# The weight products of a two-branch transformer kernel: the rows of the last chunk computed for two heads at a time, the flips of that chunk merged, and the first loads cut into halves

## The chip, the cores and the metric

The kernel runs on one core of a Trainium2 chip. The core has five engines: TensorE (matrix products; the profile shows its products as PE and its weight loads as PEld), VectorE (DVE), ScalarE (ACT), GpSimd (POOL) and SyncE (SP, which here only issues transfers). Sixteen DMA engines move data between device memory and the on-chip memory. Products are accumulated in eight banks of PSUM, and DVE or ACT copy them out. The metric is the device time of one launch in microseconds. The kernel before takes 1566.67 us, the median of three runs from 1566.27 to 1566.87.

## The reference

The input x has 2048 tokens of width 448 in bfloat16. Two kinds of layers alternate, twice each, every one of them on a layer norm of x and added to x.

```python
x = x + A(layernorm(x));  x = x + B(layernorm(x))
x = x + A(layernorm(x));  x = x + B(layernorm(x))

def A(x):                          # 64 segments of 32 tokens, one after the other
    mem = mem0                     # 8 rows
    for s in range(64):
        h = concat([mem, x[segment s]])               # 40 rows
        q, k, v = h @ Wq, h @ Wk, h @ Wv              # 16 heads of 256
        p = softmax(mask(q @ k.T * 256 ** -0.5))      # memory rows see all, others are causal
        o = (p @ v) @ Wo                              # back to 448
        mem, out[s] = o[:8], o[8:]

def B(x):                          # 448 -> 1792 -> 448
    return (relu(x @ W_gate) * (x @ W_up)) @ W_down
```

Both A layers have the same weights, and so have both B layers. Layer A is a chain: each segment needs the memory rows of the one before.

## The kernel before, in words

**Preparation.** The weights of A are multiplied with each other first. For each head, A_h = Wq_h Wk_h^T is a matrix of 448 x 448, and B_h = Wv_h Wo_h is another. The scores are then (h A_h) h^T and the output is p (h B_h). `A_sb` and `B_sb` hold these products for all 16 heads. A width of 448 is three chunks of 128 (`kd` = 0, 1, 2) and one of 64 (`kd` = 3). The heads are worked through in eight pairs: a *position* `p` is two heads, `eo` = 0 and 1, of two 128-column pieces each; `hf, p4 = divmod(p, 4)`.

In the first loop over positions (lines 378 to 413) Wq and Wk of a position lie in memory as 448 rows by 512 columns. `load_nat` (306) asks for them on SP's queue: rows 0 to 383 as one transfer, rows 384 to 447 as a second one, and again 64 rows to the other half of the partitions (those of Wq once more, or of Wv beside Wk). TensorE flips them with transposes, 128 x 128 each, into a bank `tpw` (`flips`, 327; its `half` is one unit with eight transposes), and a copy takes them to `qT` or `kT`. The part of Wv that came with Wk is copied to `v3`. The units of position p+1 are kept in `todo` and are done between the products of position p. For each `kd` and `eo` two products of 384 columns go to a bank `aps` and two of 64 columns to `mxw` (388 to 393). At `kd` = 3 these products hold the same 64 rows of A in both halves of the partitions, and the copies take 64 rows to the lower or the upper half, as the main loop wants them (`upper`, 51). All four units of position 0 stand ahead of the first product.

In the second loop (415 to 441) B_sb is made: twelve transposes of Wv a position, twelve products of 448 columns into `bps`, and one group of four products with 64 output rows each, two and two side by side in the left and right columns of the array (431 to 435). Wo comes on POOL's queue (`load_wo`, 369), with a wait that spreads it over TensorE's work (`spread`, 88).

**Who copies.** `share` (320) keeps a clock of expected ends for DVE and ACT and gives each copy to the one that would be done first. `bank` (121) takes the bank that is expected to be free longest. TensorE's instructions are tied to the order in which they are written (`in_order`, 80). DVE's and ACT's are tied to it only from the main loop on (`dve.on = act.on = True`, 1047). Before that the scheduler of the framework may order them otherwise, and it did: the statistics of the first rows of x, written behind position 1, run at 2.80 us.

**Warm-up.** `keep_warm` (173) issues products on zeros while TensorE waits for the first load: eight at the start and four between the flips of Wq and of Wk of position 0.

**Main loop.** 68 steps, two chains (the first A layer, and the second four segments behind) in one step. A step projects h with all tiles of A (`project`, 639): 28 tiles for each of the halves `hf` = 0, 1, in banks of six, six, four, six and six tiles, each bank copied out to `TQ` (tiles 0 to 23) or `TZ` (24 to 27). `EARLY` (43) says which banks take their last chunk from the lower or the upper half of the partitions, two products side by side. `scores` (759) multiplies chunks of `TQ` and `TZ` with h; the order of chunks is `KD` (46), 0, 1, 3, 2, and for both chains the first three chunks of the memory's and of the own scores stand ahead of the last (788 to 792). Then come softmax, a flip of the weights p to `PT`, the products with h (`weigh_m`, `weigh_x`) into `Y`, and those with B_sb (`project_out`). Every other step also runs a block of layer B in between.

Of the kernel before, what the change touches and what calls it, by code (L numbers as in the profile page):

```python
# [15 lines left out]
DM = 448  # L16
# [26 lines left out]
EARLY = (((0, 6), (12, 18)), ((0, 6), (12, 18)))  # L43


KD = (0, 1, 3, 2)
# [4 lines left out]
def upper(hf, t):  # L51

    return any(b <= t < b + 6 for _, b in EARLY[hf])


def tidx(kd, eo, p4):

    return kd * 8 + eo * 4 + p4 if kd < 3 else 24 + p4


def build_kernel(ctx, tc, A_x, A_mem0, A_Wq, A_Wk, A_Wv, A_Wo, B_W_gate, B_W_up, B_W_down, out,
# [31 lines left out]
    class InOrder:  # L93

        def __init__(self, eng):
            self.eng, self.last, self.on = eng, None, False

        def __getattr__(self, name):
            f = getattr(self.eng, name)

            def call(*a, **k):
                r = f(*a, **k)  # L102
                if self.on:
                    if self.last is not None:
                        tc.add_manual_dep(r.ins, self.last,
                                          mybir.DependencyInfo(mybir.DependencyClass.NoSync,
                                                               mybir.DependencyReason.DATA),
                                          reason="order of issue")
                    self.last = r.ins.name
                return r  # L110

            return call
# [55 lines left out]
    nc.sync.dma_start(xp[1][:], x_dram[0:128])  # L168
# [124 lines left out]
    with tc.tile_pool(name="pre", bufs=6) as pre:  # L293
# [3 lines left out]
        nats = []  # L297
        for i in range(6):
            t = pre.tile([P, 4, 512], BF, name=f"nat{i}", bufs=1)
            nats.append(t)  # L300
        nc.gpsimd.memset(A_sb[64:128, 3, :, 24:NT, :], 0.0)
        for t in TQ + TZ + PX + PM + YB:
            nc.gpsimd.memset(t[:], 0.0)
        nn = [0]

        def load_nat(src, p, eng):
            t = nats[nn[0] % 6]
            nn[0] += 1
            cols = slice(512 * p, 512 * (p + 1))
            eng.dma_start(t[:, 0:3, :], src[0:384, cols].rearrange("(k p) n -> p k n", p=P))  # L310
            if src is Wv:
                return t
            eng.dma_start(t[0:64, 3, :], src[384:448, cols])
            eng.dma_start(t[64:128, 3, :], (Wq if src is Wq else Wv)[384:448, cols])
            return t

# [3 lines left out]
        def share(dst, src, n, per):  # L320
# [4 lines left out]
            evac(eng, dst, src)  # L325

        def flips(src, p, name):
            nat = load_nat(src, p, nc.sync)
            o = pre.tile([P, 4, 512], BF, tag="tT", name=name, bufs=4)

            def half(e2):
                tp = bank([P, 2, 512], BF, "tpw")
                n = 3 if src is Wv else 4
                for kd in range(n):
                    for e in range(2):
                        tr(tp[:, e, kd * 128:(kd + 1) * 128],
                           nat[:, kd, (2 * e2 + e) * 128:(2 * e2 + e + 1) * 128], ident[:])
                n = DM if src is Wk else 128 * n
                share(o[:, 2 * e2:2 * e2 + 2, 0:n], tp[:, :, 0:n], 2 * n, (0.6, 0.82))
                if src is Wk:  # L340
                    share(v3[:, p, 2 * e2:2 * e2 + 2, :], tp[:, :, DM:512], 128, (0.6, 0.82))

            return o, [lambda: half(0), lambda: half(1)]

        def queue(p):
            if p < NP:
                qT, a = flips(Wq, p, "qT")
                kT, b = flips(Wk, p, "kT")
                return (qT, kT), a + b
            if p == NP:  # L350
                return flips(Wv, 0, "vT")
            return None, []
# [13 lines left out]
        keep_warm(8)  # L366
# [5 lines left out]

        ready, todo = queue(0)
        for k, u in enumerate(todo):
            if k == 2:
                keep_warm(4)
            u()
        for p in range(NP):
            hf, p4 = divmod(p, 4)
            qT, kT = ready  # L380
            ready, todo = queue(p + 1)
            mx_ps = bank([P, 4, 128], F32, "mxw")
            for kd in range(4):
                for eo in range(2):
                    aps = bank([P, 3, 128], F32, "aps")
                    for t in range(2):
                        e = 2 * eo + t
                        mm(aps[:, :, :], qT[:, e, kd * 128:(kd + 1) * 128],
                           kT[:, e, 0:384], start=(t == 0), stop=(t == 1))
                    for t in range(2):  # L390
                        e = 2 * eo + t
                        mm(mx_ps[:, kd, eo * 64:eo * 64 + 64], qT[:, e, kd * 128:(kd + 1) * 128],
                           kT[:, e, 384:448], start=(t == 0), stop=(t == 1))
                    t0 = eo * 4 + p4
                    if kd < 3:
                        share(A_sb[:, kd, hf, t0:t0 + 17:8, :], aps[:], 384, (1.28, 0.85))
                    else:
                        up = [t for t in range(3) if upper(hf, t0 + 8 * t)]
                        for rows, ts in ((slice(64, 128), up), (slice(0, 64), [t for t in range(3) if t not in up])):
                            if ts:  # L400
                                d = ts[1] - ts[0] if len(ts) > 1 else 1
                                share(A_sb[rows, 3, hf, t0 + 8 * ts[0]:t0 + 8 * ts[-1] + 1:8 * d, :],
                                      aps[rows, ts[0]:ts[-1] + 1:d, :], 128 * len(ts), (1.28, 0.85))
                    if todo and 2 * kd + eo in (0, 2, 4, 5):
                        todo.pop(0)()
            share(A_sb[:, 0:3, hf, 24 + p4, :], mx_ps[:, 0:3, :], 384, (1.28, 0.85))
            share(A_sb[0:64, 3, hf, 24 + p4, :], mx_ps[0:64, 3, :], 128, (1.28, 0.85))
# [4 lines left out]
            if p == 2:  # L412
                first_rows(xn0)

        for p in range(NP):
            hf, p4 = divmod(p, 4)
            vT = ready
            ready, todo = flips(Wv, p + 1, "vT") if p + 1 < NP else (None, [])
            wo = wos.pop(0)
            for eo in range(2):  # L420
                for kd in range(3):
# [6 lines left out]
                    if kd == 1 and todo:  # L428
                        todo.pop(0)()
            bps = bank([P, 512], F32, "bps")  # L430
            for t in range(2):
                for eo in range(2):
                    e = 2 * eo + t
                    mm(bps[64 * eo:64 * eo + 64, 0:DM], v3[:, p, e, :], wo[:, e, :],
                       start=(t == 0), stop=(t == 1), tile_position=(0, 64 * eo))
            share(B_sb[:, hf, 24 + p4, 0:DM], bps[:, 0:DM], DM, (1.28, 0.85))
# [180 lines left out]
    def tile_of(ps, hf, t, i, chains, hb, j, kds, first, last):  # L617

        n = L * len(chains)
        for kd in kds:  # L620
            mm(ps[:, i * n:(i + 1) * n], A_sb[:, kd, hf, t, :], moving(hb, j, kd, chains),
# [522 lines left out]
```

## Time and profile before

| | |
|---|---|
| median of three runs | 1566.67 us |
| the profiled execution | 1565.94 us |
| its span on the core | 1564.1 us |
| TensorE busy | 1552.9 us (99%) |
| DVE, ACT, POOL busy | 1113.5, 759.1, 77.2 us |
| first product of the first loop, `aps` | at 9.26 us |
| first product of the second loop, `bps` | at 47.64 us |
| first product of the main loop, `prj` | at 75.23 us |

How to read the lines: an engine's group of instructions has its line in the kernel, the operation, what it writes and reads by the names of the kernel (`A_sb<-aps`), the shape and the count; then busy time and the mean duration of one in ns; then idle time of the engine before them and what ended it. In the timeline the first two numbers are start and length in us. Times count from the start of the span. Helpers hide the callers: nearly all products have line 144 and nearly all copies line 102, so the names of tiles tell them apart. The shown end of a product is some 0.16 us after the next one can start, because products are pipelined; the spacing of starts is the cost. In the chain of work, each piece is a start, a length and what it was.

### The profile page before, as it was taken

How to read it: one execution, taken by the hardware profiler on the slowest of the kernel's cores; microseconds unless marked ns; L12 is line 12 of the kernel's file. 1: busy time of each engine (PE TensorE's matmuls, PEld its weight loads, DVE VectorE, ACT ScalarE, POOL GpSimd, SP SyncE). 2: the span in 40 equal slices, each digit the busy share in tenths (PEclk: the TensorE clock that was granted, in tenths of full speed). 3: DMA queues.
4: the chain of work that ended last, by engine and by line, in shares of the span. 5: the costliest groups of instructions: out<-in, count | busy, mean ns of one | idle time of the engine just before them, and what ended most of it. 6: DMA issues, size and time to landing. Idle time of an engine off the chain costs nothing.

```text
span 1564.1 us, 89359 instructions
## 1 busy us (share of the span) xinstructions
PE 1552.9 (99%) x40988; PEld 1441.7 (92%) x40988; DVE 1113.5 (71%) x3656; ACT 759.1 (49%) x2126; POOL 77.2 (5%) x172
## 2 busy tenths in 40 slices
PE   9999999999999999999999999999999999999998
PEld 6689999999999999999999999999999999999997
DVE  8756777777767777777777777677777777777765
ACT  5744454454444445544444455444544554445444
POOL 3200000000000000000000000000000000000000
PEclk9999999999999999999999999999999999999999
DMA  7620000000000000000000000000000000000000
GB/s 247 199 85 9 8 10 9 7 7 10 9 9 9 10 10 4 9 9 10 9 10 9 10 3 10 9 10 9 9 9 10 4 9 9 10 8 6 7 7 9
DMA packets 28233, 33.21 MB, mean 21 GB/s; under 512 B 4168, under 2 KB 26960, under 8 KB 27856
## 3 DMA queue, kind: packets, MB, share of 16 engines
q1 hardware_dynamic: 26608, 23.76, 5.3%
q8 instruction: 320, 5.24, 1.4%
q0 software_dynamic: 1088, 3.68, 0.7%
q14 instruction: 57, 0.47, 0.1%
q10 hardware_dynamic: 160, 0.06, 0.0%
HBM read 23.70 MB, written 1.84 MB: 16 GB/s over the span
## 4 chain that ended last, share of the span: by engine, by line
PE 98%; DVE 1%; issue 0%; DMA 0%; SPq 0%; ACT 0%; POOL 0%; DVEq 0%; ACTq 0%
PE prj L144 32%; PE ox L144 25%; PE gps L144 6%; PE ups L144 6%; PE dps L144 6%; PE o L144 5%; PE y L144 4%; PE Sx L144 3%; PE pps L152 1%; PE bps L144 1%; PE aps L144 1%; PE Sm L144 1%; PE tpw L152 1%; PE ya L144 1%; PE yb L144 1%; PE tps L152 1%
## 5 line engine op out<-in xcount | busy, mean ns | idle before, releaser
L144 PE MATMUL prj<-hT,A_sb 128*128 128x80 bf16 (+3 forms) x15232 | 550.8, 199 | 0.4 <-ACT hT L102 0.2
L144 PEld LDWEIGHTS <-A_sb 128*128 128x128 bf16 (+1 forms) x15232 | 505.0, 99 | 20.7 <-issue 1.0
L144 PEld LDWEIGHTS <-B_sb 128*128 128x128 bf16 (+1 forms) x15008 | 489.6, 103 | 13.8 <-issue 0.7
L144 PE MATMUL ox<-Y,B_sb 128*128 128x80 bf16 (+2 forms) x11256 | 443.1, 200 | 1.5 <-issue 1.5
L102 ACT CAST TQ<-prj 128x480 bf16<-128x480 f32 (+1 forms) x380 | 184.2, 497 | 101.8 <-PE prj L144 89.8
L102 DVE CAST Y<-y 128x256 bf16<-128x256 f32 x376 | 151.1, 457 | 39.4 <-PE y L144 39.2
L102 ACT ACTIVATE se<-se 128x160 f32<-128x160 f32 (+2 forms) x270 | 81.6, 302 | 195.0 <-DVE se L102 189.4
L102 ACT CAST Y<-y 128x512 bf16<-128x512 f32 (+2 forms) x392 | 136.9, 419 | 66.9 <-PE y L144 61.2
L102 DVE CAST TQ<-prj 128x480 bf16<-128x480 f32 (+1 forms) x228 | 128.6, 573 | 8.1 <-PE prj L144 7.6
L144 PE MATMUL gps<-xT,Wg_sb 128*128 128x128 bf16 (+3 forms) x1904 | 128.7, 216 | 0.0
L144 PEld LDWEIGHTS <-Wu_sb 128*128 128x128 bf16 (+1 forms) x1904 | 104.8, 97 | 5.6 <-issue 0.2
L102 ACT COPY os<-o 64x16 f32<-64x16 f32 (+3 forms) x134 | 25.5, 191 | 171.6 <-PE o L144 169.9
L144 PE MATMUL ups<-xT,Wu_sb 128*128 128x128 bf16 (+3 forms) x1632 | 106.9, 216 | 0.4 <-DVE xT L102 0.4
L144 PEld LDWEIGHTS <-Wg_sb 128*128 128x128 bf16 (+1 forms) x1904 | 106.8, 97 | 0.4 <-issue 0.4
L144 PEld LDWEIGHTS <-hk 40*128 40x128 bf16 (+1 forms) x1950 | 98.9, 96 | 8.6 <-issue 1.4
L102 DVE TENSOR_REDUCE ssum<-se 128x4 f32<-128x160 f32 (+2 forms) x270 | 73.2, 271 | 42.2 <-ACT se L102 38.5
L102 DVE SCALAR_TENSOR_TENSOR hh<-gps,ut 128x512 bf16<-128x512 f32 (+2 forms) x136 | 78.1, 594 | 34.7 <-ACT ut L102 21.7
L102 ACT CAST TZ<-prj 64x320 bf16<-64x320 f32 (+2 forms) x264 | 96.9, 377 | 8.2 <-DVE TZ L102 5.3
L144 PE MATMUL dps<-Wd_sb,hh 128*128 128x448 bf16 (+1 forms) x504 | 93.3, 343 | 0.8 <-DVE hh L102 0.8
L144 PEld LDWEIGHTS <-TQ 128*128 128x128 bf16 x1938 | 85.8, 97 | 1.3 <-ACT TQ L102 0.8
L144 PE MATMUL y<-PT,hk 40*128 40x256 bf16 (+1 forms) x1280 | 86.0, 249 | 0.0
L102 DVE CAST Y<-ya 128x256 bf16<-128x256 f32 x134 | 56.9, 425 | 39.0 <-PE ya L144 37.2
(130 smaller groups left out, 1891.4 us busy)
## 6 DMA issues: line engine op xcount, KB each, us to landing
wo<-in_A_Wo_dram POOLq DMA_DIRECT2D x8, 448.0 KB, 4.6
nat<-in_A_Wq_dram SPq DMA_DIRECT2D x8, 384.0 KB, 4.7
nat<-in_A_Wk_dram SPq DMA_DIRECT2D x8, 384.0 KB, 4.7
nat<-in_A_Wv_dram SPq DMA_DIRECT2D x8, 384.0 KB, 4.2
xa<-in_A_x_dram SPq DMA_DIRECT2D x32, 56.0 KB, 2.2
xa<-xp SPq DMA_DIRECT2D x32, 56.0 KB, 1.9
xp<-in_A_x_dram SPq DMA_DIRECT2D x30, 56.0 KB, 2.3
out_dram<-xa SPq DMA_DIRECT2D x30, 56.0 KB, 2.4
```

The lines of the kernel that those rows point to most:

```text
L102: r = f(*a, **k)
L144: in_order(nc.tensor.matmul(out, lhsT, rhs, **k))
L152: in_order(nc.tensor.transpose(out, src, idn))
```

## The change

- **Loads.** The tiles `nat` hold only the rows 0 to 383 of a position; the last 64 rows of Wq and of Wk (or of two positions of Wv) share a tile `natl`, lower and upper half. The loads of position 0 stand at the very start, in two column halves each, Wq on SP's queue and Wk on ACT's. Those of position 1 come in halves too, on SP, behind the fourth product of the warm-up (`ask_second`). From then on `ask(p + 2)` stands at the head of position p. The first load of x moves behind that of position 2.
- **Flips.** A unit is six transposes for rows 0 to 383 of two pieces (`flip`), or four for the merged last rows of Wq and Wk (`flip_last`). Position p has five units, 28 transposes where there were 32. Three of the five of position 0 stand ahead of the first product. In the second loop one more unit every other position flips the last rows of Wv for two positions.
- **Products.** `kd` = 3 is no longer in the loop. `last_rows` makes the 64 rows of both heads with four products of 448 columns, in pairs in the left and right columns of the array, so that head `eo` lies in the half `eo` of the partitions. It stands at the end of even positions and at the head of odd ones. The paired products of the second loop, `last_out`, are placed in the same manner.
- **Order of tiles.** Head `eo` of tile t follows from its bank, so the order of tiles changes in A_sb (`a_tile`), B_sb (`tidx`), `TQ`, `TZ` and in the operands of `yb` and `y2`. Banks 12 and 18 now both reach into chunk 1 of `TQ`, and `KD` becomes 0, 3, 1, 2, with two chunks ahead of the others instead of three.
- **Order of issue.** DVE and ACT follow the written order from the start. Statistics and first rows of x stand in the second loop, at positions 1 and 2.
- **Warm-up.** Four and three products, with the request for position 1 between them.

```diff
-EARLY = (((0, 6), (12, 18)), ((0, 6), (12, 18)))
-KD = (0, 1, 3, 2)
+EARLY = ((0, 6), (12, 18))
+KD = (0, 3, 1, 2)
...
+def a_tile(t):
+    if t >= 24:
+        return t
+    u = t // 12 * 6 + t % 6
+    return 3 * (t // 6 % 2 * 4 + u % 4) + u // 4
...
 def tidx(kd, eo, p4):
-    return kd * 8 + eo * 4 + p4 if kd < 3 else 24 + p4
+    return kd * 8 + p4 * 2 + eo if kd < 3 else 24 + p4
...
-                if self.on:
-                    if self.last is not None:
+                if self.last is not None:
...
-    nc.sync.dma_start(xp[1][:], x_dram[0:128])
+    nats = [pre.tile([P, 3, 512], BF, name=f"nat{i}", bufs=1) for i in range(6)]
+    nats3 = [pre.tile([P, 512], BF, name=f"natl{i}", bufs=1) for i in range(3)]
+    for e in range(2):
+        cols = slice(256 * e, 256 * e + 256)
+        for i, (eng, src) in enumerate(((nc.sync, Wq), (nc.scalar, Wk))):
+            eng.dma_start(nats[i][:, :, cols], rows3(src, cols))
+            if e == 0:
+                eng.dma_start(nats3[0][FR[i], :], src[384:448, 0:512])
...
+        def ask(p):
+            if p < NP:
+                asked[p] = ([load_nat(src, p) for src in (Wq, Wk)], load_last(((Wq, p), (Wk, p))))
+            elif p < 2 * NP:
+                asked[p] = (load_nat(Wv, p - NP),
+                            load_last(((Wv, p - NP), (Wv, p - NP + 1))) if p % 2 == 0 else None)
+
+        def ask_second():
+            for e in range(2):
+                cols = slice(512 + 256 * e, 768 + 256 * e)
+                for i, src in enumerate((Wq, Wk)):
+                    r = nc.sync.dma_start(nats[2 + i][:, :, slice(256 * e, 256 * e + 256)], rows3(src, cols))
+                    if e == i == 0:
+                        spread(r)
+                if e == 0:
+                    asked[1] = (nats[2:4], load_last(((Wq, 1), (Wk, 1))))
...
+        def flip(nat, e2, dst):
+            tp = bank([P, 2, 512], BF, "tpw")
+            for kd in range(3):
+                for e in range(2):
+                    tr(tp[:, e, kd * 128:(kd + 1) * 128],
+                       nat[:, kd, (2 * e2 + e) * 128:(2 * e2 + e + 1) * 128], ident[:])
+            share(dst, tp[:, :, 0:384], 768, (0.6, 0.82))
+
+        def flip_last(nat, dst):
+            tp = bank([P, 4, 128], BF, "tpl")
+            for e in range(4):
+                tr(tp[:, e, :], nat[:, e * 128:e * 128 + 128], ident[:])
+            share(dst, tp[:].rearrange("p e (i d) -> p e i d", i=2), 512, (0.6, 0.82))
...
-        keep_warm(8)
+        keep_warm(4)
+        ask_second()
+        keep_warm(3)
...
+        def by_heads(ps, a, b, n):
+            for t in range(2):
+                for eo in range(2):
+                    mm(ps[FR[eo], 0:n], a(2 * eo + t), b(2 * eo + t), start=(t == 0), stop=(t == 1),
+                       tile_position=(0, 64 * eo))
+
+        def last_rows(qk, hf, p4):
+            ps = bank([P, DM], F32, "apl")
+            by_heads(ps, lambda e: qk[:, e, 0, 384:DM], lambda e: qk[:, e, 1, :], DM)
+            eng = one_of(900, (1.28, 0.85))
+            for eo in range(2):
+                t0 = 3 * (eo * 4 + p4)
+                evac(eng, A_sb[FR[eo], 3, hf, t0:t0 + 3, :], ps[FR[eo], 0:384])
+            for eo in range(2):
+                evac(eng, A_sb[FR[eo], 3, hf, 24 + p4, 64 * eo:64 * eo + 64], ps[FR[eo], 384:DM])
...
         for p in range(NP):
+            qk = ready
+            ask(p + 2)
+            ready, us = queue(p + 1)
+            todo += us
+            if p == 0:
+                nc.sync.dma_start(xp[1][:], x_dram[0:128])
+            if p % 2:
+                last_rows(qk, hf, p4)
-            for kd in range(4):
-                for eo in range(2):
+            for eo in range(2):
+                for kd in range(3):
...
+            while todo:
+                todo.pop(0)()
+            if p % 2 == 0:
+                last_rows(qk, hf, p4)
...
-            if p == 1:
-                xn0 = normed(row_stats(xp[1]))
...
+            if p % 2 == 0:
+                last_out(p, wo)
+            if p == 1:
+                xn0 = normed(row_stats(xp[1]))
+            if p == 2:
+                first_rows(xn0)
...
             if i0 < 24:
-                T = TQ[hf][:].rearrange("p g u w -> p g (u w)")[:, :, 16 * i0:16 * (i0 + k)]
+                u0, eo = i0 // 12 * 6, i0 // 6 % 2
+                T = TQ[hf][:].rearrange("p g u w -> p g (u w)").rearrange("p g (t e q) -> p t e g q", e=2, q=16)
+                T = T[:, u0:u0 + 6, eo]
...
-                mem(KD[:3])
-                own(KD[:3])
-                mem(KD[3:])
-                own(KD[3:])
+                mem(KD[:2])
+                own(KD[:2])
+                mem(KD[2:])
+                own(KD[2:])
...
-                mm(yb[:, 128:192], hk[:, 3 + eo, :], PT[:, 64 * eo:64 * eo + 64], start=(eo == 0), stop=(eo == 1))
+                mm(yb[:, 128:192], hk[:, 3 + eo, :], PT[:].rearrange("p (b o q) -> p b o q", o=2, q=16)[:, :, eo, :], start=(eo == 0), stop=(eo == 1))
```

More of the change, by code (lines that the diff above doesn't have):

```diff
@@ L95, in __init__ @@
         def __init__(self, eng):
[L96 removed]
+            self.eng, self.last = eng, None
         def __getattr__(self, name):
@@ L324, in share @@
             until[eng] = ends[eng]
[L325 to L343, printed above, removed]
+            return eng
@@ L345, in queue @@
         def queue(p):
             if p < NP:
[L347 to L352, printed above, removed]
+                nat, last = asked[p]
+                qk = pre.tile([P, 4, 2, DM], BF, tag="qk", name="qk", bufs=2)
+                us = [lambda i=i, e2=e2: flip(nat[i], e2, qk[:, 2 * e2:2 * e2 + 2, i, 0:384])
+                      for e2 in range(2) for i in range(2)]
@@ L392, in build_kernel @@
[L392 to L403, printed above, removed]
@@ L627, in project_early @@
         pre = {}
-        for pair in [EARLY[hf][i] for i in pairs]:
+        for pair in [EARLY[i] for i in pairs]:
             for i0 in pair:
```

116 lines of the change are left out of this document (62 added, 54 removed).

## The prediction

> **What bounds the kernel now.** I read the page first, then busy time in stretches, then the chain of work in its first 100 us, then the timeline at the start.
>
> ```profile
> span 1564.1 us, 89359 instructions
> PE 1552.9 (99%) x40988; PEld 1441.7 (92%) x40988; DVE 1113.5 (71%) x3656; ACT 759.1 (49%) x2126; POOL 77.2 (5%) x172
> ```
>
> TensorE is busy for the whole span. The change touches mainly the preparation, so the next view is busy time by 20 us.
>
> ```profile
> 0.00:20.00 20.00, 17.59 (x186) 11.71 (x187) 13.80 (x40) 7.92 (x21) 14.44 (x28) 1.00 0.79 245
> 20.00:40.00 20.00, 20.00 (x266) 15.71 (x265) 18.46 (x41) 13.14 (x38) 0.65 (x1) 1.00 0.81 252
> ...
> 60.00:80.00 20.00, 20.00 (x316) 12.41 (x315) 14.10 (x30) 13.93 (x34) 6.92 (x8) 1.00 0.56 177
> ```
>
> The columns are PE, PEld, DVE, ACT, POOL busy, granted clock, DMA share and GB/s. TensorE is idle only in the first stretch. The chain of work gives the sizes of the pieces.
>
> ```profile
> 9.26 0.49 PE aps L144 x2
> ...
> 20.72 0.45 PE tpw L152 x8
> 21.17 0.33 PE aps L144 x2
> 21.55 0.33 PE aps L144 x2
> 21.93 0.45 PE tpw L152 x8
> ...
> 50.20 1.74 PE bps L144 x10
> 51.94 0.34 PE tpw L152 x6
> 52.28 1.14 PE bps L144 x6
> ...
> 75.23 1.40 PE prj L144 x60
> ```
>
> From 9.26 (first product of the preparation) to 75.23 (first projection of the main loop) the chain is TensorE without a break: 65.97 us. A transpose is 0.45/8 = 0.056 us, one `kd`,`eo` block of the first loop 21.55 - 21.17 = 0.38 us, a product of 448 columns 1.14/6 = 0.19 us. What precedes 9.26 is waiting:
>
> ```profile
> 1.18 0.42 SPq L310 DMA_DIRECT2D nat<-in_A_Wq_dram  x1
> 1.18 3.60 PE L144 MATMUL junk<-still 128*128 128x512 bf16 x8 [1.18 <-DVE still L171]
> 4.99 1.16 PE L152 MATMUL tpw<-ident,nat 128*128 128x128 bf16 x16 [0.21 <-DMA nat<-in_A_Wq_dram]
> 5.98 1.03 PE L144 MATMUL junk<-still 128*128 128x512 bf16 x4
> 7.59 0.51 PE L152 MATMUL tpw<-ident,nat 128*128 128x128 bf16 x6 [0.59 <-DMA nat<-in_A_Wk_dram]
> 9.26 0.49 PE L144 MATMUL aps<-kT,qT 128*128 128x384 bf16 x2 [0.27 <-DVE kT L102]
> ```
>
> All flips of position 0 stand ahead of its first product, and wait for two whole loads that SP issues one behind the other.
>
> **The change part by part.** Minus is a gain.
>
> (a) *The start, -3.2 us.* The first loads come as column halves on two queues, with x no longer ahead of them. Only three of the five flip units precede the first product. The seven junk products end at 1.18 + 7 x 0.45 = 4.3 (eight took 3.60). The first 512 KB must be there by about 4.5: the data begin near 1.8, and the stretch after that moves
>
> ```profile
> 2.00:6.00 4.00, 3.79 (x24) 1.71 (x23) 2.31 (x14) 0.01 (x1) 3.94 (x5) 1.00 0.82 248
> ```
>
> 248 GB/s, so 1.8 + 0.52/0.248 = 3.9, and somewhat later with the shorter rows of (c). Then 16 transposes (0.9) and a copy: 0.55 on DVE or 0.8 on ACT.
>
> ```profile
> L102 DVE CAST B_sb<-bps 128x448 bf16<-128x448 f32 x27 | 16.9, 625 | 5.3 <-PE bps L144 4.1
> L102 ACT CAST A_sb<-aps 128x384 bf16<-128x384 f32 x32 | 15.0, 482 | 11.0 <-PE aps L144 10.9
> L102 DVE COPY qT<-tpw 128x1024 bf16<-128x1024 bf16 x16 | 10.8, 677 | 1.4 <-PE tpw L152 1.4
> L102 DVE COPY vT<-tpw 128x768 bf16<-128x768 bf16 x10 | 5.5, 553 | 0.6
> L102 ACT COPY vT<-tpw 128x768 bf16<-128x768 bf16 x6 | 4.8, 798 | 1.1 <-PE tpw L152 1.1
> ```
>
> That puts the first product at about 6.05 instead of 9.26. The bounds are 5.9 (all there at 4.3) and 6.9 (data 0.7 late).
>
> Here a rule is weighed. The row: eight junk products of 512 columns took 3.60 us, four later ones 1.03, so the clock came to full rate only after some 3.5 us of products. The Trainium skill, "TensorE: Matmul & The Clock Gate", section "What's actually happening", says that the array runs at half rate until a free-running window of about 3.4 us was busy. Seven products are 3.15 us, under one window. If the flips, which follow at once, fill the window, some five transposes run at half rate, 0.3 us (inside my bounds); if the window is missed, a further one of 3.4 us runs at half rate and the sum is 1.7 us worse (a rival below).
>
> (b) *TensorE's work after the first product, -2.9 us.*
> - The second halves of position 0's flips now come after it: 12 x 0.056 = +0.67.
> - Positions 1 to 7 have 28 transposes instead of 32: -28 x 0.056 = -1.56.
> - The `kd` = 3 blocks go: two a position, 16 x 0.383 = -6.1. In their place come eight groups of four products in column pairs. The nearest row is the group of the second loop that is built like this already:
>
> ```profile
> 53.58 0.54 PE L144 MATMUL bps<-wo,vT 128*128 128x448 bf16 x2
> 54.05 0.57 PE L144 MATMUL bps<-wo,v 128*64 128x448 bf16 x4
> 54.56 0.36 PE L144 MATMUL bps<-wo,vT 128*128 128x448 bf16 x1
> ```
>
> Two plain products from 53.58 fill 0.38, so the group holds 53.96 to 54.56, 0.60 us: two pairs of 0.19 and 0.22 of switching. The change puts two groups side by side (the end of an even position and the start of the next), which pays the switch once: 0.60 + 0.38 = 1.0 a couple, 4.0 for four. If the switch is paid each time, it is 4.8.
> - In the second loop the last rows of Wv, which came with Wk's flips, get transposes of their own: 4 x 4 x 0.056 = +0.9; its paired groups also stand side by side: 4 x (1.2 - 1.0) = -0.8.
> - Sum: 0.67 - 1.56 - 6.1 + 4.0 + 0.9 - 0.8 = -2.9; -1.3 if no switch is saved.
>
> The copies must stay hidden. A position's TensorE work falls from 8 x 0.38 + 4 x 0.45 = 4.85 to 6 x 0.38 + 28 x 0.056 + 0.5 = 4.4 us. The copies are four flips on DVE (2.2), the merged one of 512 columns (0.43, by the slope between 768 and 1,024), seven of 384 on ACT (3.4) and last rows (two of 384 and two small, 1.4): 7.4 over two engines, 3.7 each against 4.4. Were they not hidden, each position would gain less than its 0.45.
>
> (c) *Waits for the next loads, +1.6 us.* TensorE starts 3.2 us sooner on the same DMA engines. Position 1's halves are held back until the fourth junk product (about 3 us); SP then issues six transfers for it and four for each later position, at about 0.5 each (0.42 in the first row of SP above), which keeps up. The half loads have rows of 512 bytes; no row has that size. The nearest are the packets of the first 10 us (nearly all of 1,024) and the last output rows of 448:
>
> ```profile
> q1 hardware_dynamic: 2252, 2.10, 69.2%
> ...
> q1 hardware_dynamic: 85, 0.03, 2.4%
> ```
>
> The first is 16 x 10 us x 0.692 / 2252 = 49 ns for 932 bytes, the second (from the stretch 1558 to 1564) 16 x 6 x 0.024 / 85 = 27 ns for some 353 bytes: 0.69 of the rate. So half rows run at 0.69 to 1.0 of 248 GB/s; I take 0.8, 200 GB/s. Position 0 needs 0.92 MB, and the first two 1.83 MB: 1.8 + 1.83/0.200 + 0.5 to land = 11.5, where the last flip that wants them stands at about 10.5. Whole rows then bring position 2 3.5 us later, at 15.0, against 14.5; from there the supply (3.5 a position) outruns the use (4.4). That is 1.0 + 0.5 and a little for copies that a couple of last rows waits for. At 1.0 of the rate it is 0.5, at 0.69 3.6.
>
> (d) *Orders of issue, +0.3 us.* DVE and ACT are now held to program order from the start, and the statistics of x stand in the second loop. DVE must there wait for two POOL operations before it goes on, with its copies queued behind:
>
> ```profile
> 13.21 0.23 POOL L255 TENSOR_SCALAR rstd<-mv 128x1 f32<-128x1 f32 x1
> 13.83 0.57 POOL L256 TENSOR_TENSOR rstd<-rstd,half 128x1 f32<-128x1 f32 x1
> ```
>
> That is 0.8 and two hand-overs, about 1.0 us once. Eight banks at 0.38 are 3 us of cover, so 0 to 1.0; I take 0.3. On SP the later x load waits for that too, with Wv loads behind it that are wanted some 7 us later: nothing.
>
> (e) *The main loop, 0.* The order of tiles in A, B, TQ and the weights is renamed, with as many products. One thing moves: chunk 1 of the scores now needs the last copied bank, so the wait for it stands at the third chunk instead of the fourth.
>
> ```profile
> 701.44 0.56 ACT L102 CAST TQ<-prj 128x480 bf16<-128x480 f32 x1 [0.37 <-PE prj L144]
> ...
> 701.81 0.24 PE L144 MATMUL Sm<-hT,TQ 128*128 128x80 bf16 x2
> ...
> 702.22 0.20 PE L144 MATMUL Sm<-hT,TQ 128*128 128x80 bf16 x1
> ...
> 1541.34 0.42 ACT L102 CAST TQ<-prj 128x48 bf16<-128x48 f32 x2 [0.25 <-PE prj L144]
> ...
> 1541.81 0.14 PEld L144 LDWEIGHTS <-TQ 128*128 128x128 bf16 x3 [0.20 <-ACT TQ L102]
> ```
>
> The copy ends at 702.00, its reader starts at 702.22. Three chunks took 0.41, so the reader moves 0.137 forward, to 0.085 behind the copy. A hand-over from ACT took 1541.81 - 1541.76 = 0.05 where TensorE did wait, and weights load about 0.02 ahead of their product. It fits, by about 0.01. Bounds: 0, and 0.1 us x 60 steps = 6 if the copy into spaced columns is that much longer.
>
> Sum: -3.2 - 2.9 + 1.6 + 0.3 = -4.2. The profiled execution took 1565.94 us (1.84 beside its span), 0.73 under the median of 1566.67. So 1561.7 for such an execution, and 1562.5 on the scale of the median.
>
> **The rivals.**
> 1. *Starved start.* Half rows at the low end, (c) 3.6 and (d) 1.0: -1.5, so 1565.2. For it: DMA share is already 0.79. Against: the rate was 248 GB/s from 2 us on.
> 2. *The clock misses its window*: 1.7 us on the sum, 1564.2. The flips directly behind the junk products speak against it.
> 3. *The last copy of TQ decides* (slower). Every copy into TQ writes runs of 16 elements at twice the spacing. From 0.01 us more on that copy TensorE waits in each step; at 0.08 a step the gain is gone, at 0.19 (a 0.56 us copy turned into 0.75) it costs 60 x 0.18 = 10.8, and the time is 1573. Against: a copy jumps every 16 elements already.
> 4. *Short runs in the moving operand* (slower). The odd and even products of `yb` and `y2` now read 16 elements, skip 16. At half rate that is four of 64 and eight paired of 128 columns a step, 0.11 + 0.21, 20 us in all: 1583. The shortest run in this trace is 40, so nothing here shows it. The Trainium skill, "SBUF — State Buffer", section "Door 1: The DMA port swizzle", has lines of 16 bytes, which runs of 32 bytes fill; no run here shows that.
> 5. *Nothing arrives*: what the main loop starts with comes no earlier, and the gain is given back there: 1566.5.
>
> **How the numbers follow.** Forecast 0.60 (its own range 1561.0 to 1563.5), rival 1 0.17, rival 2 0.05, rival 3 0.09, rival 4 0.03, rival 5 0.06. About what a measurement can tell from no change is 0.2%, 3.1 us. Only the forecast is faster by more than that: 0.60. Rivals 1, 2 and 5 are within it: 0.28. Rivals 3 and 4 are slower: 0.12. The low end is the best sum, -3.2 - 2.9 + 0.5 = -5.6, with one more microsecond for an unexplained gap in the first step that may go: 1560.0. The high end takes in rivals 1, 2 and 5: 1566.8.
>
> **What would show it.** First `aps` near 6 us; first `prj` near 71; about 1.0 us for two `apl` groups side by side; waits for `nat` in positions 1 and 2 of 1 to 2 us; DVE under 90% in 20 to 40. In the main loop no wait on TQ at the third chunk, and a step that takes what it took. It is wrong if the first `aps` comes after 7, if `nat` is waited for beyond position 3, or if any wait recurs in each step.

## The result, and the profile after

The changed kernel takes 1560.67 us in the median (1560.22 to 1561.34, six runs) against 1566.41 for the kernel before, measured beside it. The ratio is 0.9965, with a 95% interval from 0.9952 to 0.9977: faster by 0.35%, 5.7 us in the medians (3.6 to 7.5 us by the interval). The two profiled spans differ by 5.0 us.

The page of the changed kernel, its span and busy times:

```profile
span 1559.1 us, 89243 instructions
PE 1547.9 (99%) x40935; PEld 1438.6 (92%) x40935; DVE 1110.6 (71%) x3651; ACT 762.8 (49%) x2119; POOL 77.6 (5%) x173
```

Busy time in stretches of the changed kernel (columns as before: PE, PEld, DVE, ACT, POOL, granted clock, DMA share, GB/s):

```profile
20.00:40.00 20.00, 20.00 (x255) 14.89 (x254) 17.16 (x37) 15.76 (x37) 1.50 (x2) 1.00 0.85 267
...
5.90:71.15 65.25, 64.14 (x686) 42.80 (x687) 53.16 (x109) 47.65 (x100) 21.06 (x29) 1.00 0.76 241
```

TensorE still has no gap between 20 and 40 us, and DVE is down from 18.46 to 17.16. The last row runs from the first product of the first loop to the first projection: 65.25 us where it was 65.97, with 1.11 us in which TensorE is idle.

TensorE's timeline at the places that matter (start, length, instruction, idle time before it):

```profile
1.18 3.17 PE L146 MATMUL junk<-still 128*128 128x512 bf16 x7 [1.18 <-DVE still L186]
4.16 0.97 PE L154 MATMUL tpw<-ident,nat 128*128 128x128 bf16 x12
...
5.90 0.48 PE L146 MATMUL aps<-qk 128*128 128x384 bf16 x2 [0.51 <-DVE qk L105]
6.22 0.22 PE L146 MATMUL mxw<-qk 128*128 128x64 bf16 x2
6.93 0.51 PE L154 MATMUL tpw<-ident,nat 128*128 128x128 bf16 x6 [0.49 <-DMA nat<-in_A_Wq_dram]
...
8.38 0.50 PE L154 MATMUL tpw<-ident,nat 128*128 128x128 bf16 x6
8.88 0.48 PE L146 MATMUL aps<-qk 128*128 128x384 bf16 x2
...
11.35 1.39 PE L146 MATMUL apl<-qk 128*64 128x448 bf16 x8
12.67 0.50 PE L146 MATMUL aps<-qk 128*128 128x384 bf16 x2
...
17.71 0.22 PE L146 MATMUL mxw<-qk 128*128 128x64 bf16 x2
18.16 0.51 PE L154 MATMUL tpw<-ident,nat 128*128 128x128 bf16 x6 [0.23 <-DMA nat<-in_A_Wk_dram]
...
51.04 1.68 PE L146 MATMUL bps<-wo,vT 128*128 128x448 bf16 x8
53.02 0.57 PE L146 MATMUL bps<-wo,v 128*64 128x448 bf16 x4 [0.30 <-DVE B_sb L105]
53.52 0.40 PE L154 MATMUL tps<-ident,xn 128*128 128x128 bf16 x4
```

The start is at 5.90 instead of 9.26. Six waits are left. Two small products of 0.03 each begin at 6.22, so the flip at 6.93, which needs position 0's own second half of Wq, is 0.65 late. By the same reckoning the flip at 18.16 (position 3) is 0.39 late, and one at 13.90 (position 2, a line not shown here) 0.12. Six flips take 0.34, so the product at 8.88 is 0.16 late: it waits for a copy. The first couple of groups of last rows takes 1.32 from its start to the next product (11.35 to 12.67), where the later ones take 0.88: 0.44 late, for a copy too. Eight products of 0.19 from 51.04 end at 52.56, and a paired group starts 0.09 behind plain products in any case (53.96 to 54.05 in the kernel before), so the group at 53.02 is 0.37 late.

The chain of work of the changed kernel (start, length, what):

```profile
21.09 0.88 PE apl L146 x8
21.97 0.43 PE aps L146 x2
...
71.15 1.40 PE prj L146 x60
```

Two groups side by side take 0.88, and 0.10 more stands in the first product behind them (0.43 where two take 0.33). One of the eight couples does not stand side by side: in the second loop the flips of x (`tps` at 53.52 in the timeline above) come between its two groups.

The preparation thus ends at 71.15 instead of 75.23: 4.08 us. Where is the rest of the 5.0? Not in the steps of the main loop. The timeline around `kps`, which every step has once, shows the 21st and the 61st of them, in the kernel before

```profile
497.04 0.36 PE L144 MATMUL kps<-ident,hT 128*128 128x128 bf16 x4
...
1393.71 0.36 PE L144 MATMUL kps<-ident,hT 128*128 128x128 bf16 x4
```

and in the changed one

```profile
492.10 0.36 PE L146 MATMUL kps<-ident,hT 128*128 128x128 bf16 x4
...
1388.77 0.36 PE L146 MATMUL kps<-ident,hT 128*128 128x128 bf16 x4
```

896.67 us for forty steps in both. The rest is gaps of TensorE in the first steps, which wait for nothing that the profile shows. The chain of the kernel before:

```profile
84.43 1.03 issue
...
88.64 0.55 issue
...
103.42 0.93 issue
```

The chain of the changed kernel:

```profile
78.42 0.48 issue
...
82.18 0.71 issue
...
97.27 0.39 issue
```

2.51 against 1.58: 0.93 us, what is missing. The prediction had such a gap only as one more microsecond at its low end. That the change made it is not shown. The changed kernel, its repeat and the ten experiments below that leave the main loop as it is take between 420.95 us (the profile above) and 423.15 us from the first projection to the 21st `kps`. The one profile of the kernel before, with 421.81, lies among them.

### The profile page after: what moved, and what is told of

It is laid out like the page before. It is cut to its first block, busy times and chain, and to the rows that moved or that the text cites. A ratio compares the mean times of both kernels' runs of the same rounds, so it can differ in the third digit from the quotient of the medians.

```text
span 1559.1 us, 89243 instructions
## 1 busy us (share of the span) xinstructions
PE 1547.9 (99%) x40935; PEld 1438.6 (92%) x40935; DVE 1110.6 (71%) x3651; ACT 762.8 (49%) x2119; POOL 77.6 (5%) x173
## 4 chain that ended last, share of the span: by engine, by line
PE 98%; DVE 1%; DMA 1%; issue 0%; POOL 0%; ACT 0%; SPq 0%; DVEq 0%; POOLq 0%
PE prj L146 32%; PE ox L146 25%; PE gps L146 6%; PE ups L146 6%; PE dps L146 6%; PE o L146 5%; PE y L146 4%; PE Sx L146 3%; PE pps L154 1%; PE bps L146 1%; PE Sm L146 1%; PE ya L146 1%; PE yb L146 1%; PE tps L154 1%; PE aps L146 1%; PE tpw L154 1%
## 5 line engine op out<-in xcount | busy, mean ns | idle before, releaser
L270 POOL TENSOR_SCALAR rstd<-mv 128x1 f32<-128x1 f32 x66 | 14.7, 223 | 1407.5 <-DVE mv L105 1335.8
```

The source lines that it names most:

```text
L270: nc.gpsimd.tensor_scalar(out=rstd[:], in0=mv[:, 1:2], scalar1=EPS, scalar2=None, op0=ALU.add)
```

## The experiments

All are edits of the changed kernel. Ratios are to the kernel before, run beside each. Their intervals are some 2 us wide to either side, so apart from one experiment (the last copy of TQ) no ratio tells an experiment from the changed kernel; what each edit does is read from its profile. Two profiles of the changed kernel differ by 0.22 us in their first projection, so a few tenths in one profile prove nothing.

**The start of the old kernel.**

```diff
-    for e in range(2):
-        cols = slice(256 * e, 256 * e + 256)
-        for i, (eng, src) in enumerate(((nc.sync, Wq), (nc.scalar, Wk))):
-            eng.dma_start(nats[i][:, :, cols], rows3(src, cols))
...
+    for i, src in enumerate((Wq, Wk)):
+        nc.sync.dma_start(nats[i][:], rows3(src, slice(0, 512)))
+        nc.sync.dma_start(nats3[0][FR[i], :], src[384:448, 0:512])
...
-        for _ in range(3):
+        for _ in range(5):
             todo.pop(0)()
```

> The changed kernel with the start of the old one: position 0's loads whole, one behind the other on SP's queue, and all five flip units ahead of the first product (x stays behind). Theory (the start is what the halves on two queues buy): the first aps comes at about 8.3 instead of 5.90, 0.67 us of flips is then already done, and the waits for nat behind it (1.0 us in the changed kernel) vanish, so the first prj comes at 71.1 + 2.4 - 0.67 - 1.0 = 71.8 and the run is 0.7 us longer. Rival (the transfers are the limit, the halves only move the wait): the first prj stays at 71.1 within 0.2. Other rival (the start is worth its full 3.2 us): the first prj at 74.

Its timeline at the start:

```profile
4.19 0.82 PE L154 MATMUL tpw<-ident,nat 128*128 128x128 bf16 x6
6.38 0.82 PE L154 MATMUL tpw<-ident,nat 128*128 128x128 bf16 x6 [1.37 <-DMA nat<-in_A_Wk_dram]
...
8.70 0.80 PE L146 MATMUL aps<-qk 128*128 128x384 bf16 x2
```

Its chain of work:

```profile
71.80 1.40 PE prj L146 x60
```

The first product comes 2.8 us later, the first projection 0.65 us later (expected 0.7). The ratio is 0.9964 (0.9954 to 0.9975), the same as that of the changed kernel. So by this profile the halves on two queues move the start by 2.8 us and the end of the preparation by 0.65: the rest is given back, as two units of flips that then stand behind the first product (0.67), and as waits for loads and copies, which this execution hardly has before the second loop.

**The last copy of TQ, one chunk further forward.**

```diff
-KD = (0, 3, 1, 2)
+KD = (0, 1, 3, 2)
...
-                mem(KD[:2])
-                own(KD[:2])
-                mem(KD[2:])
-                own(KD[2:])
+                mem(KD[:1])
+                own(KD[:1])
+                mem(KD[1:])
+                own(KD[1:])
```

> The changed kernel with the chunk that needs the last copied bank moved one further to the front: chunk order 0, 1, 3, 2, and one chunk of memory and own scores ahead of it instead of two. Theory (the reader of the last copy of TQ stands 0.142 us behind the copy in plain steps and 0.087 in steps with a block of layer B, and a hand-over takes 0.05 with the weight load 0.02 ahead): moving it 0.137 further leaves 0.005 and -0.050, so TensorE waits 0.07 in 30 steps and 0.12 in 30, 5.8 us longer in all. Rival (there is more cover than the rows show, or a copy starts earlier): within 1 us of the changed kernel.

First the timeline of the changed kernel in a step with a block of layer B and in a plain step, copies on ACT and readers on TensorE:

```profile
696.50 0.56 ACT L105 CAST TQ<-prj 128x480 bf16<-128x480 f32 x1 [0.37 <-PE prj L146]
...
697.14 0.23 PE L146 MATMUL Sm<-hT,TQ 128*128 128x80 bf16 x2
...
722.27 1.26 ACT L105 CAST TQ<-prj 128x480 bf16<-128x480 f32 x2 [0.29 <-PE prj L146]
...
723.67 0.23 PE L146 MATMUL Sm<-hT,TQ 128*128 128x80 bf16 x2
```

Then the experiment, the timeline around its `kps` and in the same step:

```profile
494.26 0.36 PE L146 MATMUL kps<-ident,hT 128*128 128x128 bf16 x4
...
725.14 1.26 ACT L105 CAST TQ<-prj 128x480 bf16<-128x480 f32 x2 [0.29 <-PE prj L146]
...
726.46 0.21 PE L146 MATMUL Sm<-hT,TQ 128*128 128x80 bf16 x1
...
1393.81 0.36 PE L146 MATMUL kps<-ident,hT 128*128 128x128 bf16 x4
```

In the changed kernel the reader starts 0.08 behind the end of the copy in the first (696.50 + 0.56 = 697.06) and 0.14 in the second (722.27 + 1.26 = 723.53). In the experiment it starts 0.06 behind it: it waits. Forty steps take 899.55 instead of 896.67, 0.072 a step in the mean (0.07 and 0.12 were expected in the two kinds of steps, 0.095 in the mean). The ratio is 0.9993 (0.9984 to 1.0002), no longer told apart from the kernel before: this one order of chunks eats nearly the whole gain. So a last copy that ends too late holds TensorE up in every step, as the third rival says; the change stops just short of it. What the rival gave as the reason, a longer copy into spaced columns, did not happen: the copy takes 0.56 in both kernels.

**Groups apart.** `last_rows` and `last_out` at the end of every position, so that none stand side by side.

```diff
-            if p % 2:
-                last_rows(qk, hf, p4)
...
-            if p % 2 == 0:
-                last_rows(qk, hf, p4)
+            last_rows(qk, hf, p4)
```

> The changed kernel with each paired group of products at the end of its own position, so that none stand side by side. Theory (a switch between whole and half columns costs 0.2 us a group and is paid once a couple): the first prj comes 8 x 0.2 = 1.6 us later, at 72.7. Rival (the switch is no cost of its own, the array only drains): within 0.3 of 71.1.

Its chain:

```profile
16.25 0.50 PE apl L146 x4
...
72.01 1.40 PE prj L146 x60
```

The first projection is 0.86 later, not 1.6; the ratio is 0.9972 (0.9962 to 0.9983). One group takes 0.50 and two take 0.88, so a couple saves 0.12 there and 0.09 more ahead of the group: 0.2 a couple, as expected. But the other waits are about 1.1 us shorter in this execution: the stall inside the first couple (0.44) and the wait near 18 (0.39) are gone. The price of the switch was right; that shorter waits would pay for a part of it was left out.

**Ordered by head.**

```diff
-            for t in range(2):
-                for eo in range(2):
+            for eo in range(2):
+                for t in range(2):
                     mm(ps[FR[eo], 0:n], a(2 * eo + t), b(2 * eo + t), ...
```

> The changed kernel with the four products of a paired group ordered by head, so that left and right columns no longer alternate. Theory (two products in left and right columns run at the same time only if they follow each other): of the four only the middle two can overlap, so each of the 16 groups takes one more product, 0.19 us, and the first prj comes 3.0 us later, at 74.1. Rival (no overlap at all when ordered by head): 6 us later, 77. Other rival (pairs never overlapped): no change.

The chain of this kernel:

```profile
21.63 0.88 PE apl L146 x8
...
71.71 1.40 PE prj L146 x60
```

Eight products take 0.88, as when left and right alternate; in the trace they start in pairs 7 ns apart, as before some 3 ns, and the next pair 0.19 later. My theory fell: the order in which the four are written does not matter. The first projection is 0.56 later, but not for the groups: the start is 0.21 later, and the waits near 14 and 18 are longer (0.56 and 0.62). Taken alone this would fit "pairs never overlapped", so that was tried directly. The ratio is 0.9968 (0.9955 to 0.9981).

**Full columns instead of pairs.** The last rows of A by products of 128 columns, of which 64 are thrown away, one bank for each head.

```diff
-            by_heads(ps, lambda e: qk[:, e, 0, 384:DM], lambda e: qk[:, e, 1, :], DM)
+            for eo in range(2):
+                ps = bank([P, DM], F32, "apl")
+                for t in range(2):
+                    mm(ps[:, 0:DM], qk[:, 2 * eo + t, 0, 320:DM], qk[:, 2 * eo + t, 1, :], ...
```

> The changed kernel with the last rows of A made by four products of the full 128 columns (64 of them thrown away) instead of four side by side, in two banks. Theory (it is the running side by side that brings the gain of the first loop): a group takes 4 x 0.19 = 0.76 us instead of 0.50 with its share of the switching, so eight take 2.1 us more and the first prj comes at 73.2. Rival (the gain is that 448 columns are one product instead of 384 and 64, and that flips are fewer): 71.1 within 0.4.

Its chain:

```profile
30.15 1.51 PE apl L146 x8
...
72.64 1.40 PE prj L146 x60
```

Eight products take 1.51 against 0.88 side by side: 0.63 a couple, 2.5 us for four, less the switching that falls away. The preparation ends 1.5 later (2.1 expected; the start is 0.16 later, and the waits for loads and copies are some 0.9 shorter, 0.44 of it the stall in the first couple). The ratio is 0.9972 (0.9961 to 0.9982). The pairs do overlap, and this part carries the largest single piece of the gain that was tried alone.

**The statistics of x earlier.**

```diff
+            if p == 4:
+                st0 = row_stats(xp[1])
...
-                xn0 = normed(row_stats(xp[1]))
+                xn0 = normed(st0)
```

> The changed kernel with the statistics of the first rows of x (and with them the two POOL operations) at position 4 of the first loop; only the two operations that use them stay at position 1 of the second. Theory (DVE, held to program order, stands still for POOL, which first issues a load of Wo that waits for TensorE): the gap of 0.46 us in TensorE at 52.4 goes, and the first prj comes at 70.6. Rival (the gap is the two operations on DVE themselves, 0.6 us): it stays, within 0.15.

The changed kernel, the timeline of POOL and DVE at that place:

```profile
50.08 0.75 POOL L417 DMA_DIRECT2D wo<-in_A_Wo_dram  x1 [2.89 <-PE bps L146]
...
51.83 0.61 DVE L105 TENSOR_SCALAR xn<-xp,mv,rstd 128x448 bf16<-128x448 bf16 x2 [1.01 <-POOL rstd L271]
```

The experiment, TensorE's timeline at its first flips and at that place:

```profile
4.23 1.46 PE L154 MATMUL tpw<-ident,nat 128*128 128x128 bf16 x12
...
51.35 1.68 PE L146 MATMUL bps<-wo,vT 128*128 128x448 bf16 x8
52.96 0.57 PE L146 MATMUL bps<-wo,v 128*64 128x448 bf16 x4
```

DVE had stood still for 1.01 us; with the statistics earlier TensorE goes through without a gap. So the theory holds for the gap. The first projection still comes at 71.09, since the start of this execution was slower: twelve flips in 1.46 instead of 0.97, first product at 6.34, and 0.6 instead of 0.4 waited for `nat` at 17.7. The ratio is 0.9962 (0.9948 to 0.9976).

**Loads of position 1 all held back, or not at all.**

```diff
-                    if e == i == 0:
-                        spread(r)
+                    spread(r)
...
-                    asked[1] = (nats[2:4], load_last(((Wq, 1), (Wk, 1))))
+                    asked[1] = (nats[2:4], load_last(((Wq, 1), (Wk, 1)), spread))
```

> The changed kernel with all six loads of position 1 behind the fourth junk product; in the changed kernel only the first of the six carries the wait, and two of the others were issued ahead of it. Theory (these two, 260 KB, run beside the second halves of position 0, for which TensorE waits 0.65 us at 6.3): the second halves land 0.7 to 1.0 us sooner, that wait goes, position 1 lands at about the same 9.6, and the first prj comes at 70.6. Rival (all transfers share what the DMA engines give, so the wait only moves to position 1 or 2): the first prj within 0.2 of 71.1.

Held, all six loads behind the fourth junk product: the first projection comes at 71.61, half a microsecond later, and the ratio is 0.9969 (0.9957 to 0.9981). Position 0's second halves did not land sooner (7.2 and 8.3 instead of 6.9 and 7.1). They were issued at 1.86, and SP, free of position 1, issued a whole load of position 2 (384 KB) right behind them, at 2.48.

```diff
-                    if e == i == 0:
-                        spread(r)
```

> The changed kernel without the wait of position 1's loads: they follow those of position 0 at once. Theory (position 0's second halves are delayed by what runs beside them, what comes later is earlier): the wait at 6.3 grows from 0.65 to about 0.9 us, position 1 lands 0.8 sooner at 8.8, the wait at 17.7 (0.39) goes, so the first prj stays within 0.3 of 71.1. Rival (holding them back is what makes the start quick): the first aps at 6.5 or later and the first prj above 71.8.

Free, none of them held: first projection at 71.25 and ratio 0.9966 (0.9953 to 0.9979), no difference from the changed kernel. By these profiles holding all of them costs about 0.4 us and holding none costs nothing. That the loads share what the DMA engines give fits both and is not shown by itself.

**Both of the harmless ones**, free loads and early statistics.

> The changed kernel with both: position 1's loads follow at once, and the statistics of x stand at position 4 of the first loop. Theory (the gap of 0.46 us at 52 is DVE standing still, the waits for nat are shared out by the DMA engines): no gap at 52, a wait of about 0.6 us for nat near 17.7, first prj near 70.8, so 0.3 us less than the changed kernel. Rival (the two stand in each other's way): first prj at 71.1 or later.

First projection at 71.05, no gap at 52, 0.4 waited at 17.9; the ratio is 0.9963 (0.9950 to 0.9975). That is not told apart from the changed kernel by this measurement.

**The first load of x later**, with the same two edits; its statistics stand at position 6.

```diff
-            if p == 0:
+            if p == 4:
                 nc.sync.dma_start(xp[1][:], x_dram[0:128])
```

> As the kernel with both, but the first load of x is asked for at position 4 of the first loop and its statistics are made at position 6. Theory (SP has eight landings to wait on; the loads of x that it takes among those of positions 2 and 3 use two of them up, and position 3's Wk is issued only when position 2's has landed, at 13.9): with the load of x away, position 3 is issued and lands 0.3 to 0.5 us sooner, and the wait near 17.7 shrinks below 0.3 us. Rival (the wait is the rate of the DMA engines or the landing of position 2 alone): it stays between 0.4 and 0.7 us.

Inconclusive by itself. In the trace SP still issues the load of x at 9.4 us: it waits for nothing, so the framework's scheduler put it there again. The wait near 18.0 is 0.45, the first projection 71.22, the ratio 0.9966 (0.9953 to 0.9978). Position 3's Wk is issued at 14.18, right behind the landing of position 2's at 14.11. That landing as such is not the condition: with the first load of x ahead of everything (the last experiment) position 3's Wk is issued at 11.57, and position 2's lands at 13.02. What holds in all fourteen traces is the theory's limit: SP never has more than eight loads in flight. In this trace seven are in flight when position 2's Wk lands, and position 3's is issued 0.07 later.

**The changed kernel again.**

> The changed kernel once more, unchanged. Theory (the gaps of TensorE in the first three steps of the main loop, 1.6 us for which the profile shows no releaser, are chance, and so is 0.9 us of the 5.0 that its span was shorter): they come out between 1 and 4 us and at other places, the first prj within 0.4 of 71.1, and the steps after the fifth within 0.02 us. Rival (they belong to the kernel): the same gaps at the same places within 0.2 us.

Its chain of work:

```profile
70.93 1.40 PE prj L146 x60
...
78.28 0.31 issue
...
81.88 0.71 issue
...
97.20 0.67 issue
```

Its timeline at the first flips:

```profile
4.25 0.84 PE L154 MATMUL tpw<-ident,nat 128*128 128x128 bf16 x12
```

The gaps of the first steps come at the same places, with 1.69 us in all instead of 1.58, so "at other places" was wrong. Their single sizes differ by up to 0.28, though, and the way from the first projection to the 21st `kps` takes 421.38 us instead of 420.95: of the 0.9 us by which the kernel before was slower there, the repeat gives half back. The ratio is 0.9965 (0.9953 to 0.9978), as the first time.

**The first load of x ahead of everything.**

```diff
+    nc.sync.dma_start(xp[1][:], x_dram[0:128])
     prepare = ExitStack()
...
-            if p == 0:
-                nc.sync.dma_start(xp[1][:], x_dram[0:128])
```

> The changed kernel with the first load of x (112 KB) ahead of everything on SP's queue again. Theory (the start is bound by SP's issue and by bytes): Wq's first half lands 0.45 us later, the first aps comes at 6.3 to 6.5, and as the waits behind it shrink the first prj stays within 0.4 of 71.1. Rival (every delay of the start is paid in full): the first prj at 71.6.

First product at 6.58, first projection at 71.34; the ratio is 0.9968 (0.9956 to 0.9980). A start that is 0.7 us later costs 0.2 at the end, no more than two profiles of one kernel differ by. With this load away from among those of positions 2 and 3, position 3's Wk lands at 16.66 instead of 18.11, and the wait near 18 is gone, which is what the experiment with the later load was meant to show.

## Why the prediction was right

The forecast was 1562.5 us; 1560.67 was measured, inside the range and faster by more than 0.2%, but 0.3 us below the forecast's own range of 1561.0 to 1563.5. Of the 1.8 us between forecast and measurement, 0.9 are the first steps' gaps. About 1.0 more comes from the scale (the preparation gave 0.1 less than forecast): the profiled execution of the kernel before lay 0.73 under its median, which the forecast added back, and that of the changed kernel lies 0.23 over its own. No run shows more than chance in either. Term by term, in us to the end of the preparation:

| step | predicted | measured | from |
|---|---|---|---|
| (a) start | -3.2 | -3.36 | first `aps` 9.26 to 5.90 |
| (b) TensorE's work | -2.9 | -2.85 | 65.25 - 65.97, less the waits below |
| (c) waits for loads and copies | +1.6 | +1.76 | 0.65, 0.12 and 0.39 for `nat`, 0.16 and 0.44 for copies |
| (d) DVE waits for POOL | +0.3 | +0.37 | group at 53.02 |
| (e) steps of the main loop | 0 | 0 | 896.67 for forty steps in both |
| sum | -4.2 | -4.1 | first `prj` 75.23 to 71.15 |
| first steps' gaps | none | -0.9 | 2.51 to 1.58, one profile each |

- (a) was right in size and in place. It is worth little by itself: undone, it costs 0.65 in the profile, and nothing that the run times tell. Nothing in the sum said so, because (a) and (c) are two halves of one thing: a start brought forward against the same supply of data.
- (b): a couple of groups takes 0.98 with the first product behind it, as worked out from 0.60 and 0.38. The full-column run shows that running side by side is what it lives on. The measured -2.85 is what remains when all waits are taken off. One saving of the sum did not come: the couple in the second loop that the flips of x part pays the switch twice, 0.2 us.
- (c) came out at its size, but not where it was expected, and in this it was luck. It was sized by half rows at 0.8 of the rate, as waits of positions 1 and 2. The two first halves landed 3.4 and 3.7 us after their issue, and all of position 1 by 9.55, sooner than the 11.5 that I had; no flip of that profile waits for it. The largest wait is for position 0's own second halves, beside which two of position 1's loads ran (issued at 2.47 and 3.00; only one of the six is held back). The wait at 18.16 is for position 3: with seven loads in flight on SP its load is issued only at 13.91, when position 2's has landed (13.85). And 0.60 of the 1.76 is for copies, of which the sum had only "a little".
- (d) held in its mechanism (1.01 us of DVE behind two POOL operations and a load issue) and nearly in its size.
- (e): the reader of the last copy was to move to 0.085 behind it in the step that the prediction shows. It stands 0.08 behind it in a step of that kind and 0.14 in a plain one. The third rival is real as far as the order goes: 0.137 further and it costs 2.9 us in forty steps. The fourth, slow reading of runs of 16, is excluded by the equal steps.
- The second rival, the clock, happened in part of the runs: twelve flips took 0.84 and 0.97 in the two profiles of the changed kernel, and 1.46 in that of the early statistics. Less the 0.16 by which an end is shown late, that is 0.057 a flip at 0.84 and 0.108 at 1.46: half the rate. It moves the first product by 0.4, not by the 1.7 of the rival, and is taken up by the wait for the next halves. With the old loads and the new warm-up, six flips still took 0.82 at 6.4. This agrees with the rule of the Trainium skill, "TensorE: Matmul & The Clock Gate", section "What's actually happening", that the window runs free: where it falls decides. The granted clock in the busy-time rows reads 1.00 throughout and does not show it.
- What the sum lacked are the gaps of the first three steps. Between the two profiles they changed by 0.9 us, but the same main loop varies by 2.2 us there from one profile to the next, so it is not shown that the change shortened them. Their cause stays open.

## What to carry to other kernels

A start that is brought forward is worth only what the supply behind it allows: look at when the second and third loads land, not only at the first product. Before an operand's last copy is used one product sooner, subtract the two times in the profile: here 0.08 to 0.14 us were left, a hand-over took 0.06, and one more step of the same kind ate nearly all of a gain of 5 us. Half-width products side by side pay when groups stand together, since going to the half width and back cost about 0.2 us each time here.

## What the runs showed of the hardware that was not expected

- Four products in left and right columns take the same time whether written alternating or head by head (0.88 us for eight in both). They start in pairs, 3 ns apart in the first case and 7 ns in the second; the trace does not tell which columns a product uses, so in which order they ran is not shown.
- SP has at most eight loads in flight in every one of the fourteen traces. With seven in flight and an eighth just landed, the next issue followed 0.06 to 0.07 us behind the landing (13.85 to 13.91, 14.11 to 14.18).
- Warm-up products may end before the clock is up. With seven of 512 columns the flips behind them ran at full or at half rate from one execution to the next (0.84 and 0.97 us for twelve in the changed kernel, up to 1.46 with the same start).
- TensorE has 1.6 to 2.5 us of gaps in the first three steps after the preparation, for which the profile names no releaser. In two profiles of one kernel they come at the same places, but not at the same sizes.
